# One step's issue order in a fused causal attention and soft-MoE kernel: first scores and maxima's transpose to the front, attention products to the end

## The chip, the cores and the metric

The kernel runs on one core of a Trainium2 chip. The metric is device time in microseconds (us) of one execution. A core has a tensor engine (TensorE; PE in the profile, its weight loads PEld), a vector engine (VectorE, DVE), a scalar engine (ScalarE, ACT), GpSimd (POOL) and a queue that issues DMAs (SyncE, SP). Each engine takes its instructions in the order of the program and waits on semaphores for what the others make. SBUF is the on-chip memory, PSUM the memory that TensorE writes to; it has eight banks of 2 KB a partition.

## The reference

Causal attention over 8 batches of 12 heads, 448 positions, head dimension 64; then a soft mixture of experts over the 3584 tokens with 32 slots and 8 experts.

```python
scores = q @ k^T / sqrt(64)            # above the diagonal: -1e9
attn   = softmax(scores); x = attn @ v # x as (3584, 768)
logits = x @ phi                       # (3584, 32)
d = softmax(logits, over tokens); slot_input = d^T @ x
slot_out[e] = relu(slot_input[e] @ w1[e]) @ w2[e]
out = softmax(logits, over slots) @ slot_out
```

## The kernel before

There are 96 heads, taken in 48 pairs. The main loop (line 510) has one step i a head; h is 0 in even steps and 1 in odd ones, p is the pair. A step works on four heads at once, at different stages, and the order in which it issues their parts is written out by hand in the tuple ORDER (line 47), one row for even steps and one for odd ones; the loop walks it (line 539). Since every engine is in order, the place of a name in ORDER says what it stands behind on its own engine, and nothing else. These are the names, by engine:

- TensorE: c0, c3, c12 and k0 to k3 are the first scores of head i+2, a causal mask and four passes into a PSUM tile s of two banks (scores1). mr0 is the transpose of the maxima of head i+1 into the tile rt (max_row). t0 to t3 are four more passes into the tile s of head i, which add the rounding remainder of q and take off the row's maximum (scores2). a0 to a3 are the attention products of head i-1: ten products of 128x128 by 128x65 into the one tile po, two passes each (attv).
- VectorE: x0 to x3 find the maxima of head i+2 in blocks, first with one large transposing reduction over s (x0), then with three small elementwise maxima inside the tile r (max_keys). mr1 reduces rt to the row maxima mr of head i+1. n0 to n2 divide the product of head i-1 by its sum and write it to x (norm).
- GpSimd: sp spreads mr over the remainder tile r2 (max_spread). sk, in even steps, and sq, in odd ones, take the rounded copy off k and q of pair p+2, 64x896 values each (sub_k, sub_q).
- ScalarE: exp makes the probabilities pt of head i. ck and cq (even steps) make the rounded copies ks and qd of pair p+2, c2 (odd steps) copies ks to k2. ld takes the exponentials of a batch's logits.

The name plan runs what is due in the step from a table of due steps (line 433). Twelve steps are a batch. In a batch there are six transposes of x, one a pair (xtrans: four TensorE transposes into a tile xt, one ScalarE copy); three logits items (sixteen small TensorE passes into g, then lt on VectorE, in the third also the batch's maximum bm and the running maximum run_m); one item with the transposes of the exponentials and logits and three ScalarE instructions (logits_e); and two dispatches (eight TensorE passes into sp, one VectorE instruction into si).

The tiles s have three buffers, so the first scores of head i+2 wait for exp of head i-1. The tiles rt, xt, g, tp and sp share a single PSUM bank (misc, line 209): each waits until the one before it in the program has been read. po is one tile as well.

SP loads the queries and keys of pair p+3 and the values of pair p+1 at the head of an odd step (lines 512 to 516), into buffers that sk and sq set free, and one tile of expert weights in every second odd step. The loop is followed by the end of the attention, then by the experts and the output, whose weights are loaded while they run.

Of the kernel before, what the change touches and what calls it, by code (L numbers as in the profile page):

```python
# [20 lines left out]
PPB = NH // 2  # L21
# [23 lines left out]


ORDER = (
# [4 lines left out]
)  # L52

SC0, SC1, SC2, SC3 = 512, 0, 320, 960
# [30 lines left out]
def attention_soft_moe(ctx: ExitStack, tc: tile.TileContext, qk, va, phi, w1, w2, out):  # L85
# [39 lines left out]
    def load_qk(p, a, hs=slice(0, 2)):  # L125
        if p < NPAIR:
            if hs.start == 0:

                st["raw", a, p] = (wres.tile([P, 2 * WN], F32, tag="w", name=f"qk{a}_{p}")[:, 0:2 * S]
                                   .rearrange("p (h s) -> p h s", h=2)  # L130
                                   if (p, a) in ((1, 0), (2, 1)) else
                                   raw.tile([P, 2, S], F32, tag="qk", name=f"qk{a}_{p}"))
            nc.sync.dma_start(out=st["raw", a, p][:, hs], in_=qk[p, :, a, hs])

    def loads_v(p, eng=nc.sync):
        if p < NPAIR:
            eng.dma_start(out=va_[p % 2], in_=va[p])
# [28 lines left out]
    def load_w(n):  # L166
        if n < len(order):
            m, e, h, u = order[n]
            t = wtiles[order[n]] = slot(n, f"w{n}")
            src, q = (w1 if m == 0 else w2)[e, h], place(n)  # L170
            if n <= NBUF or q >= RES - 1:
                nc.sync.dma_start(out=t, in_=src[:, WN * u:WN * u + WN])
            elif u:

                nc.sync.dma_start(out=twos[n - q, q // 2], in_=src)
# [33 lines left out]
    def misc(name):  # L209
        return ps_1.tile([P, 512], F32, tag="m", name=name)  # L210
# [61 lines left out]
    def scores1_all(i):  # L272
        for part in ("c0", "k3", "c3", "c12", "k2", "k1", "k0"):
            scores1(i, part)
# [36 lines left out]
    def scores2(i, cs):  # L311
        if i >= NHD:
            return
        p, h = divmod(i, 2)
        s = st["s", i]
        k2, r2 = k2_, r2_[p % NR]
        for c in cs:
            w, m = S - CQ0[c], min(P, S - P * c)
            nc.tensor.matmul(s[0:m, SCOL[c]:SCOL[c] + w], k2[:, h, P * c:P * c + m],
                             r2[:, h, CQ0[c]:S], start=False, stop=True, skip_group_check=True)  # L320
# [41 lines left out]
    def xtrans(p):  # L362
        x = st.pop(("x", p))
        pt = misc(f"xt{p}")
        for c in range(NCH):
            nc.tensor.transpose(out=pt[:, P * c:P * c + P], in_=x[:, c], identity=ident)
        xt = st["xt", p] = xtp.tile([P, 512], F32, tag="xt", name=f"xts{p}", bufs=2)
        nc.scalar.activation(out=xt, in_=pt, func=AF.Copy)
# [13 lines left out]
    def logits_b(b, l):  # L382
        bm = st["bm", b] = moe.tile([P, 1], F32, tag="bm", name=f"bm{b}", bufs=2)
        nc.vector.tensor_reduce(out=bm, in_=l, axis=AX.X, op=ALU.max, negate=True)

        mo, mn = run_m[(b + 1) % 2], run_m[b % 2]
        nc.vector.tensor_tensor(out=mn, in0=mo, in1=st.pop(("bm", b)), op=ALU.min)

    def logits_d(b, l):
        mo, mn = run_m[(b + 1) % 2], run_m[b % 2]  # L390
        al = st["al", b] = moe.tile([P, 1], F32, tag="al", name=f"al{b}", bufs=2)
        bs = st["bs", b] = moe.tile([P, 1], F32, tag="bs", name=f"bs{b}", bufs=2)
        nc.scalar.activation(out=gs, in_=l, func=AF.Exp, bias=mn[:, 0:1], accum_out=bs)
        nc.scalar.activation(out=al, in_=mo, func=AF.Exp, scale=-1.0, bias=mn[:, 0:1])
# [5 lines left out]
    def logits_e(b):  # L400
        tp = misc(f"tp{b}")
        nc.tensor.transpose(out=tp[:, 0:P], in_=gs, identity=ident)
        nc.tensor.transpose(out=tp[:, P:2 * P], in_=lt, identity=ident)
        st["dn", b] = gs.rearrange("p (c s) -> p c s", s=NSLOT)
        nc.scalar.activation(out=gs, in_=tp[:, 0:P], func=AF.Copy)
        nc.scalar.activation(out=lg[:, b], in_=tp[:, P:2 * P], func=AF.Copy)
        nc.scalar.activation(out=run_z, in_=run_z, func=AF.Identity, scale=st["al", b][:, 0:1],
                             bias=st.pop(("bs", b))[:, 0:1])
# [15 lines left out]
    def next_logits(b, j, m):  # L424
        logits_a(b, (j, j + 1), m[:, 0:P])
        logits_t(j, m[:, 0:P])

    def dispatch(b, hf):
        sp = misc(f"sp{b}_{hf}")
        dispatch_a(b, hf, sp)  # L430
        dispatch_b(b, hf, sp)

    plan = {}
    for b in range(NB):
        o, last = 12 * b, b == NB - 1
        for j, r in enumerate((3, 5, 9, 10, 12, 13)):
            if not last or j < PPB - 2:
                plan[o + r] = lambda p=b * PPB + j: xtrans(p)
        for j, r in ((0, 8), (2, 11)):
            plan[o + r] = lambda b=b, j=j: next_logits(b, j, misc(f"g{b}_{j}"))  # L440
        if not last:
            plan[o + 14] = lambda b=b: (next_logits(b, 4, misc(f"g{b}_4")), logits_b(b, lt))
            plan[o + 16] = lambda b=b: logits_e(b)
            plan[o + 18] = lambda b=b: dispatch(b, 0)
            plan[o + 19] = lambda b=b: dispatch(b, 1)

# [63 lines left out]
    for i in range(NHD):  # L510
        p, h = divmod(i, 2)
        if h:
            load_qk(p + 3, 1)
            if p + 1 < NPAIR - 1:
                loads_v(p + 1)
            load_qk(p + 3, 0)
            if p % 2 and nload < RES:
                load_w(nload)
                nload += 1
        if i == NHD - 3:  # L520

            loads_v(NPAIR - 1, nc.scalar)
        if i < 2:
            scores2(i, (1, 0, 2))
            if i:
                scores1_all(3)
            scores2(i, (3,))
            exps(i)
            if i == 0:
                max_row(1, 0)  # L530
                warm(START[4], po0.rearrange("p a b->p (a b)")[:, 0:P])
                max_row(1, 1)
                sub_k(1, h1, nc.vector)
                max_spread(1)
                sub_q(1, h1)

        qs = [int(n[1]) for n in ORDER[h] if n[0] == "a"]
        first = qs[:2] if qs[0] == 3 else qs[:1]
        for n in ORDER[h]:
            if i < 2 and (n == "exp" or n[0] in "kt" or n in ("c0", "c3", "c12")):  # L540
                continue
            if i == 0 and n in ("mr0", "mr1", "sp"):
                continue
            if n[0] == "k" or n in ("c0", "c3", "c12"):
                scores1(i + 2, n)
            elif n[0] == "t":
                scores2(i, (int(n[1]),))
            elif n[0] == "a":
                attv(i - 1, (int(n[1]),), first)
            elif n[0] == "x":  # L550
                max_keys(i + 2, int(n[1]))
            elif n[0] == "n":
                norm(i - 1, int(n[1]))
            elif n in ("mr0", "mr1"):
                max_row(i + 1, int(n[2]))
            elif n == "ld":
                if i % 12 == 3 and i > 12:
                    logits_d(i // 12 - 1, lt)
            elif n == "plan":
                if later and i:  # L560
                    later.pop(0)()
                plan.get(i, int)()
            else:
                {"exp": lambda: exps(i), "sp": lambda: max_spread(i + 1),
                 "ck": lambda: cast_k(p + 2), "sk": lambda: sub_k(p + 2), "cq": lambda: cast_q(p + 2),
                 "c2": lambda: copy_k2(p + 1), "sq": lambda: sub_q(p + 2)}[n]()
        if i == NHD - 1:

            scs.close()
            pe = att.enter_context(tc.tile_pool(name="pe", bufs=1, space=PSUM, reuse_waits="tile"))  # L570
            ps = [pe.tile([P, 512], F32, name=f"e{k}") for k in range(6)]

    i, b, p = NHD - 1, NB - 1, NPAIR - 1
# [68 lines left out]
    for hf in range(2):  # L642
        tps = po0.rearrange("p a b->p (a b)")[:, 0:96] if hf == 0 else ps[2][:, 0:96]
        for c in range(3):
            o = 384 * hf + P * c
# [153 lines left out]
    n = NBUF  # L799
# [83 lines left out]
```

## Time and profile before

| | us |
|---|---|
| median of three runs | 467.58 |
| lowest and highest run | 467.29 and 470.31 |
| profiled execution | 467.8 |
| its span, first to last instruction | 466.0 |
| busy ScalarE, of the span | 288.5 |
| busy GpSimd, of the span | 266.7 |

All numbers of the profile are of that one execution. In a row of a timeline stand the start in us from the span's start, the duration, the engine, a line (here always a helper's, L69, so that groups are told apart by the tiles), the operation, its output and inputs, their shapes and the count; in brackets the idle time ahead of it and what ended it. The chain of waits has the start, the duration and the engine with its tile. A group's row ends with its busy time, the mean duration in ns, and its idle time. A matmul's row includes the time in which it drains, which overlaps the next one.

### The profile page before, as it was taken

To read this page: it belongs to the slowest core of one execution; us is meant where nothing else is said; L and a number is where in the kernel's file an instruction comes from. 1 tells how busy PE (TensorE), PEld (TensorE's weight loads), DVE (VectorE), ACT (ScalarE), POOL (GpSimd) and SP (SyncE) were. 2 spreads that over 40 slices of the span, in tenths; PEclk is the share of its full clock that TensorE was granted. 3 is DMA by queue.
4 is the path that set the end of the run, shared out by engine and by line. 5 is a ranking of instruction groups with operands and counts; after the bars stand their busy time and mean duration, and the time that the engine had idled before them with its cause. 6 is when DMAs were issued, how large, how long until landed. Compare 5 with 4: busy or idle time off the path is not lost.

```text
span 466.0 us, 11818 instructions
## 1 busy us (share of the span) xinstructions
PE 429.8 (92%) x4628; PEld 368.3 (79%) x4628; DVE 338.5 (73%) x954; ACT 288.5 (62%) x400; POOL 266.7 (57%) x216
## 2 busy tenths in 40 slices
PE   7799999999999999999999999999999999899850
PEld 3688998898999899988998899889988864454430
DVE  6888788878787888788788877887888447634350
ACT  5576777577767777777677677767774411243240
POOL 5788777776777677767776777677765100000000
PEclk9999999999999999999999999999999999999995
DMA  7376666765676656755676656765667999999998
GB/s 265 105 244 218 201 220 210 234 210 183 207 244 234 208 181 211 239 207 190 213 245 224 201 184 219 229 227 184 232 210 243 403 367 426 423 422 413 404 391 346
DMA packets 34471, 119.02 MB, mean 255 GB/s; under 512 B 3824, under 2 KB 8944, under 8 KB 32880
## 3 DMA queue, kind: packets, MB, share of 16 engines
q1 hardware_dynamic: 34272, 118.01, 71.8%
q8 instruction: 36, 0.59, 0.5%
q10 hardware_dynamic: 144, 0.27, 0.2%
q14 instruction: 19, 0.16, 0.1%
HBM read 107.25 MB, written 11.01 MB: 254 GB/s over the span
## 4 chain that ended last, share of the span: by engine, by line
PE 69%; DVE 14%; DMA 12%; issue 1%; ACT 1%; SPq 0%
PE po L69 31%; PE s L69 21%; DMA w<-in_w_dram 11%; DVE r L69 7%; PE xt L69 5%; PE sp L69 2%; DVE run_m L69 2%; PE g L69 2%; PE rt L69 2%; PE pp L69 1%; PE e L69 1%; DVE x L69 1%; DVE sm L69 1%; PE hp L69 1%; DMA qk<-in_qk_dram 1%
## 5 line engine op out<-in xcount | busy, mean ns | idle before, releaser
L69 PE MATMUL po<-va,pt 128*128 128x65 f32 x1900 | 193.3, 250 | 0.2 <-ACT xts L69 0.2
L69 PEld LDWEIGHTS po<-va,pt 128*128 128x128 f32 x1900 | 190.6, 170 | 0.5 <-ACT xts L69 0.4
L69 ACT ACTIVATE pt<-s 128x1024 f32<-128x1024 f32 x96 | 98.4, 1025 | 87.0 <-PE s L69 84.5
L69 DVE TRANSPOSE_TENSOR_REDUCE r<-s 128x32 f32<-128x1024 f32 x96 | 119.9, 1249 | 26.5 <-PE s L69 23.9
L69 POOL TENSOR_SCALAR_AFFINE_SELECT r<-mr 14x448 fp32r<-14x448 f32 x96 | 62.1, 646 | 86.9 <-DVE mr L69 60.4
L69 POOL TENSOR_TENSOR r<-qk,qd 64x896 fp32r<-64x896 f32 (+1 forms) x50 | 101.4, 2027 | 6.6 <-ACT qd L69 2.8
L69 POOL TENSOR_TENSOR ks<-qk,ks 64x896 fp32r<-64x896 f32 (+1 forms) x47 | 97.7, 2080 | 3.7
L69 PE MATMUL s<-r,k 128*128 128x320 f32 (+3 forms) x384 | 82.9, 297 | 2.2 <-POOL r L69 2.1
L69 PE MATMUL s<-qd,ks 128*128 128x448 f32 (+3 forms) x384 | 76.0, 308 | 0.9 <-ACT qd L69 0.8
L69 DVE TENSOR_TENSOR r<-r 128x10 f32<-128x10 f32 (+2 forms) x288 | 58.7, 204 | 9.8
L69 PEld LDWEIGHTS s<-r,k 128*128 128x128 f32 (+1 forms) x384 | 59.9, 176 | 5.8 <-POOL r L69 3.5
L69 PEld LDWEIGHTS s<-qd,ks 128*128 128x128 f32 (+1 forms) x384 | 55.1, 181 | 2.4 <-ACT qd L69 1.8
L69 ACT ACTIVATE ks<-qk 128x896 fp32r<-128x896 f32 (+1 forms) x50 | 45.7, 916 | 3.9 <-DMA qk<-in_qk_dram 2.7
L69 ACT ACTIVATE k<-ks 64x896 fp32r<-64x896 f32 (+1 forms) x49 | 45.8, 935 | 1.2
L69 ACT ACTIVATE qd<-qk 128x896 fp32r<-128x896 f32 (+1 forms) x50 | 45.7, 913 | 0.4 <-DMA qk<-in_qk_dram 0.3
L69 DVE TENSOR_TENSOR x<-po,sm 128x256 f32<-128x256 f32 x95 | 40.3, 425 | 3.3
L69 PEld LDWEIGHTS <-identb 128*128 128x128 bf16 x339 | 29.2, 99 | 16.5 <-issue 14.7
L69 PE MATMUL s<-tri,identb 128*128 128x64 bf16 (+2 forms) x288 | 39.8, 235 | 0.0
L69 PE MATMUL xt<-ident,x 128*128 128x128 f32 x188 | 29.9, 282 | 7.7 <-DVE mr L69 7.4
L69 ACT ACTIVATE xts<-xt 128x512 f32<-128x512 f32 x47 | 28.1, 597 | 11.5 <-PE xt L69 9.7
L69 DVE TENSOR_SCALAR sm<-po 128x4 f32<-128x4 f32 x95 | 15.1, 159 | 23.1 <-PE po L69 22.7
L69 DVE TENSOR_REDUCE mr<-rt 14x32 f32<-14x128 f32 x96 | 26.7, 278 | 2.5 <-PE rt L69 2.2
(135 smaller groups left out, 365.9 us busy)
## 6 DMA issues: line engine op xcount, KB each, us to landing
qk<-in_qk_dram SPq DMA_DIRECT2D x94, 448.0 KB, 3.3
w<-in_w_dram SPq DMA_DIRECT2D x43, 768.0 KB, 6.3
w<-in_w_dram SPq DMA_DIRECT2D x10, 1536.0 KB, 18.9
va<-in_va_dram SPq DMA_DIRECT2D x47, 260.0 KB, 3.4
out_dram<-ot SPq DMA_DIRECT2D x16, 384.0 KB, 6.7
out_dram<-ot SPq DMA_DIRECT2D x2, 1536.0 KB, 9.2
qk<-in_qk_dram SPq DMA_DIRECT2D x4, 224.0 KB, 3.4
hw<-in_w_dram SPq DMA_DIRECT2D x1, 768.0 KB, 6.3
```

The lines of the kernel that those rows point to most:

```text
L69: return self._tc.keep_in_program_order(op(*args, **kwargs))
```

## The change

The two rows of ORDER are written anew. On each engine:

- TensorE: first scores, then mr0 (before: among the attention products), then t0 to t3 without a break (before: t3 behind a3, or a3 and t3 apart), then what is new under pa, then a0 to a3 in one block (before: a0 and a3 ahead of mr0, a2 and a1 behind it), then plan.
- VectorE: mr1, x0 to x3, n0 to n2, plan (before: x0 to x3, mr1, n0 to n2, plan).
- GpSimd: sp, then sk or sq, the same order as before. sp follows mr1, which now stands ahead of x0.
- ScalarE, even steps: ck, exp, pa, cq, ld (before: ck, exp, cq, ld, plan). Odd steps: exp, c2, pa, ld (before: exp, ld, c2, plan).

The name pa runs a second table, plan_a, to which the six transposes of x and logits_e move; logits and dispatches stay in plan at the step's end. No instruction is added, removed or resized.

```diff
 ORDER = (
-    ("c3", "c0", "k3", "c12", "k1", "k0", "k2", "t0", "t2", "t1", "a0", "a3", "t3", "ck",
-     "mr0", "exp", "x0", "a2", "x1", "x2", "x3", "mr1", "a1", "cq", "sp", "n0", "sk", "n1", "ld", "n2", "plan"),
-    ("c3", "c0", "k3", "c12", "k0", "k1", "k2", "t0", "t1", "t2", "a0", "x0", "t3", "a3", "exp", "mr0",
-     "x1", "x2", "x3", "mr1", "sp", "a2", "a1", "n0", "ld", "n1", "n2", "sq", "c2", "plan"),
+    ("ck", "c3", "c0", "k3", "c12", "k1", "k0", "k2", "mr0", "mr1", "sp", "sk", "t0", "t2", "t1", "t3", "exp", "pa",
+     "x0", "x1", "x2", "x3", "cq", "a0", "a1", "a2", "a3", "n0", "n1", "n2", "ld", "plan"),
+    ("c3", "c0", "k3", "c12", "k0", "k1", "k2", "mr0", "mr1", "sp", "t0", "t1", "t2", "t3", "sq", "exp", "c2", "pa",
+     "x0", "x1", "x2", "x3", "a0", "a1", "a2", "a3", "n0", "n1", "n2", "ld", "plan"),
 )
...
-    plan = {}
+    plan, plan_a = {}, {}
...
-                plan[o + r] = lambda p=b * PPB + j: xtrans(p)
+                plan_a[o + r] = lambda p=b * PPB + j: xtrans(p)
...
-            plan[o + 16] = lambda b=b: logits_e(b)
+            plan_a[o + 16] = lambda b=b: logits_e(b)
...
+            elif n == "pa":
+                plan_a.get(i, int)()
             elif n == "plan":
```

## The prediction

> **What bounds the kernel now.** I read the page first (span, engine shares, the chain), then busy time by stage, the chain in order of time over two batches, the waits, and last the timelines of VectorE (DVE) and GpSimd (POOL) one by one.
>
> ```profile
> span 466.0 us, 11818 instructions
> ...
> PE 429.8 (92%) x4628; PEld 368.3 (79%) x4628; DVE 338.5 (73%) x954; ACT 288.5 (62%) x400; POOL 266.7 (57%) x216
> ...
> PE 69%; DVE 14%; DMA 12%; issue 1%; ACT 1%; SPq 0%
> ```
> ```profile
> 200.00:240.00 40.00, 38.97 (x425) 36.10 (x425) 32.29 (x96) 29.34 (x38) 29.05 (x23) 1.00 0.65 217
> ...
> 400.00:466.00 66.00, 45.65 (x408) 23.95 (x400) 23.79 (x54) 20.30 (x49) 0.00 (x0) 0.90 0.99 399
> ```
> The columns of the second view are the stage, its length, busy time of PE, weight load, DVE, ACT and POOL, granted clock, DMA share, GB/s. In the loop TensorE is busy 38.97 of 40 us; after it DMA is full (0.99), and the change leaves that stage and its bytes alone. So what the loop loses or gains goes one for one into the span.
>
> ```profile
> 161.10 0.66 PE xt L69 x4
> ...
> 194.52 1.14 PE s L69 x10
> 195.66 0.19 PE po L69 x2
> 195.85 0.03 PE s L69
> 195.88 0.50 PE po L69 x8
> 196.38 0.11 PE rt L69
> 196.49 1.06 PE po L69 x10
> 197.56 0.48 PE xt L69 x4
> 198.03 1.17 PE s L69 x10
> ...
> 199.98 1.08 PE po L69 x10
> ...
> 205.73 0.04 issue
> 205.77 0.66 PE xt L69 x4
> ```
> ```profile
> PEld xt L69 <- DVE mr L69: 9.8, 16, 1.2
> ```
> ```profile
> L69 DVE TENSOR_TENSOR run_m<-run_m,bm x7: 1284/1285/1303, 68.2 to 336.5; 128x1 f32<-128x1 f32 x7
> ```
> The chain in order of time shows a step of nothing but TensorE: from 194.52 to 198.03, 3.51 us. Two like points one batch of twelve steps apart, 161.10 and 205.77, give 44.67 us a batch, 3.72 a step. In between, once a batch, the chain leaves TensorE: the last product stands at 199.98, and the transpose of x at 205.77 waits for the maxima's reduction (mr). The row of waits prices it at 1.2 us at most (9.8 us in all); the row of run_m, seven of them, says it comes seven times.
>
> **The change, by engine, and its price.** The row of a batch's stall first, in VectorE's own order (start, duration):
>
> ```profile
> 201.50 0.42 DVE L69 TENSOR_TENSOR x<-po,sm 128x256 f32<-128x256 f32 x1
> 201.84 0.28 DVE L69 TENSOR_TENSOR lt<-g,lt 128x128 f32<-128x128 f32 x1
> 202.15 0.29 DVE L69 TENSOR_REDUCE bm<-lt 128x1 f32<-128x128 f32 x1
> 202.47 1.28 DVE L69 TENSOR_TENSOR run_m<-run_m,bm 128x1 f32<-128x1 f32 x1
> 203.68 1.24 DVE L69 TRANSPOSE_TENSOR_REDUCE r<-s 128x32 f32<-128x1024 f32 x1
> 204.95 0.56 DVE L69 TENSOR_TENSOR r<-r 128x10 f32<-128x10 f32 x3
> 205.44 0.28 DVE L69 TENSOR_REDUCE mr<-rt 14x32 f32<-14x128 f32 x1
> 205.65 0.14 DVE L69 TENSOR_SCALAR sm<-po 128x4 f32<-128x4 f32 x1
> ...
> 206.03 0.43 DVE L69 TENSOR_TENSOR x<-po,sm 128x256 f32<-128x256 f32 x1
> ```
> ```profile
> 201.64 2.10 POOL L69 TENSOR_TENSOR ks<-qk,ks 64x896 fp32r<-64x896 f32 x1
> 205.79 0.64 POOL L69 TENSOR_SCALAR_AFFINE_SELECT r<-mr 14x448 fp32r<-14x448 f32 x1 [2.05 <-DVE sm L69]
> 206.51 2.11 POOL L69 TENSOR_TENSOR r<-qk,qd 64x896 fp32r<-64x896 f32 x1
> ```
> A one-column run_m takes 1.28 us and ends at 203.75; POOL's subtraction ends at 203.74. That is a wait on POOL, not work. The same early in the loop with x1, the first of the three small maxima that follow the large transposed one (x0):
>
> ```profile
> 43.05 1.58 DVE L69 TENSOR_TENSOR r<-r 128x10 f32<-128x10 f32 x1
> ```
> ```profile
> 42.51 2.09 POOL L69 TENSOR_TENSOR r<-qk,qd 64x896 fp32r<-64x896 f32 x1
> ```
> ```profile
> 44.95 0.28 DVE L69 TENSOR_REDUCE mr<-rt 14x32 f32<-14x128 f32 x1
> ```
> ```profile
> L69 DVE TENSOR_TENSOR r<-r 128x6 f32<-128x6 f32 x54 | 9.0, 166 | 1.9
> ...
> L69 DVE SCALAR_TENSOR_TENSOR si<-si,al,sp 128x384 f32<-128x384 f32 x8 | 4.9, 615 | 0.2
> ```
> x1 should cost about what x2 costs, 0.17 us; it takes 1.58 and ends at 44.63, POOL's subtraction at 44.60. Both blocked instructions read two SBUF operands. The row at 201.50, with one operand in PSUM, keeps its 0.42 us although POOL's subtraction starts inside it. The Trainium skill, page "SBUF — State Buffer", section "Who interferes with whom", says that a DVE instruction with two SBUF inputs and a GpSimd instruction that reads SBUF exclude one another, and that the one issued later waits for the whole of the other. The trace agrees for VectorE as the later one, in the two places above; no row there shows POOL as the later one. By that rule the sum below stays as it is, and it is issue order that decides it.
>
> POOL and VectorE together: the term that decides. Before, mr and with it the spread (sp) and the subtraction (sk or sq) stand behind x1 to x3, so the subtraction runs over the normalisation and the next x0, and is just over when the next x1 comes. The change puts mr ahead of x0. Count from the start of mr, by the rows from 205.44: sp starts at 0.35, the subtraction at 1.07 and ends at 3.18 (206.51 plus 2.11). VectorE starts x0 at 0.21, and x1 1.27 later (203.68 to 204.95), so at 1.48. That is 0.41 inside the subtraction, which is there in every step: sk in even steps, sq in odd ones. x1 is held to 3.18. From there the rest of x1, x2 and x3 take 0.35 (44.60 to 44.95), the three normalisation instructions 0.38 from first to third (205.65 to 206.03) and the third 0.34 until the next may start (201.50 to 201.84). The next mr stands behind them on VectorE: 3.18 + 0.35 + 0.38 + 0.34 = 4.25 us a step. TensorE's 3.51 fits inside, so VectorE and POOL become the bound. Queued behind x1 are x2, x3, the normalisation, the plan's item and the next mr; the next maxima's transpose on TensorE waits for x3, and the transpose of x for mr.
>
> What the plan's items add. The scratch bank that rt needs is now released by the item before it. A logits item adds lt behind the normalisation (0.28), then release, transpose and hand-over. The transpose's row is this:
> ```profile
> L69 PE MATMUL rt<-ident,r 128*14 128x128 f32 x53 | 14.5, 275 | 0.0
> ```
> With 0.04 for each hand-over (the row at 205.73), that is 0.28 + 0.04 + 0.28 + 0.04 = 0.64, twice a batch. The third one has bm and run_m behind lt: 0.31 + 0.32 (201.84 to 202.47) and a run_m that finds POOL idle, taken at 0.17 like x2: 0.80. A dispatch item has 0.615 in place of 0.28: 0.97, twice. The x transposes add nothing: ACT empties that bank under the next first scores. Sum 2 x 0.64 + 0.80 + 2 x 0.97 = 4.02 a batch.
>
> TensorE. Of the twenty narrow passes a step, ten take 1.06, or 0.106 each, behind a rt of 0.11 that covers their first weight load. In the new order all twenty follow the last subtracted pass (0.03), too short to cover it, or a transpose of x (0.48), which does. One load more in the open costs up to 0.11 a step, nothing where x is transposed there; the widest block of score passes gains from standing together by at most the same. I take +0.05 if TensorE is the bound, and nothing here, since it has 4.25 - 3.51 = 0.74 to spare; without that cover it costs 0.05 x 91 = 4.6 us. The old stall (1.2 us, seven times) goes, for the transpose of x no longer waits behind run_m, x0 and the three maxima; what is late in its place is x1.
>
> ACT, SP, and the moved copies. exp, the k2 copy, the two casts and the copies of transposed x only change places on ACT, which is busy 62%; cq comes behind one copy more, and its reader (sq) runs a step later. If that cover went, it would be one copy in one step of two. The loads on SP's queue are not in the order; their buffers come free at the end of sk and sq, which stay 3.18 behind mr, and the row
> ```profile
> qk<-in_qk_dram SPq DMA_DIRECT2D x94, 448.0 KB, 3.3
> ```
> says 3.3 us to land, under a step of 4.25, with the reader more than a step away. Cost nothing from either side.
>
> Sum. A batch: 12 x 4.25 + 4.02 = 55.02 against 44.67, so +10.35. Subtractions are issued in steps 1 to 91. Steps 12 to 91 are 80/12 batches: +69.0. Steps 1 to 11 hold two logits items and no dispatch: (4.25 + 2 x 0.64/11 - 3.72) x 11 = +7.1. Together +76 on the profiled execution, which took 467.8 (span 466.0 and 1.8 around it): 543.8. That execution is 0.2 above the median of the three runs, so I say 543.6.
>
> **Rivals.** It gets faster. Mechanism: sk and sq start after x1 has started, and then POOL waits some 0.2 us for it and VectorE for nothing. The point from which it decides: the subtraction must start more than 1.48 behind mr instead of 1.07. Then the old stall goes and TensorE pays 4.6: 467.8 - 7 x 1.2 + 4.6 = 464.0; with the load hidden after all, 459.4. Nothing in the rows delays the subtraction by 0.41, since its operands are cast a step earlier. Only one step in two is held. If sk had to wait for its cast or load in even steps, these would stay near TensorE's (44.67 - 1.2)/12 = 3.62 and odd ones take 4.25; with half of the 4.02 a batch is 6 x 3.62 + 6 x 4.25 + 2.01 = 49.2, +4.6 a batch over 91/12 batches: 503. Against it: the landing time above, and a longer step gives the cast more room. Held, and longer still. If VectorE's small instructions follow one another end to start, not overlapped, the three places where I took an overlap (mr to x0 is under POOL's time; x3, normalisation, next mr) cost about 0.2 more a step: +18, 562. A lower clock would belong here too; the loop stood at 1.00, and TensorE would still be busy some 3.5 of 4.6 us.
>
> **How the numbers follow.** The held x1 in every step has 0.84, one step in two 0.06, not held 0.10 (0.04 faster by over 1%, 0.06 within). About 1% is what a measurement here can tell from no change. The forecast is that of the likeliest case, 544. Its own range goes from 0.17 a step less (the seven small instructions between x1 and the next mr close up by the length of one: 528) to the end-to-start case and a little clock (568). That leaves out the other two cases, 0.16, and little else. Slower by over 1%: 0.90; within: 0.06; faster: 0.04.
>
> **What would show it.** Right: x1's rows lengthen from about 0.2 us to some 1.6 and each ends with a POOL subtraction; run_m falls from 1.28 to about 0.2; batches stand 55 us apart; the longest waits in the loop are TensorE's for VectorE (rt for r, xt for mr), and its busy share in the loop falls from 97% to about 80%. Wrong: x1 short while the subtraction runs, a subtraction that starts behind x1, or mr waiting for TensorE and not for the normalisation.

## The result, and the profile after

The changed kernel takes 547.66 us (median; 546.21 to 548.26) against 467.9 for the kernel before (median of four runs), a ratio of 1.169 with a 95% interval of 1.164 to 1.174. It is slower by 80 us, and the forecast was 543.6. The profiled execution has a span of 546.1 us.

The page of the changed kernel: engine shares, then VectorE's costliest group (busy time, mean in ns, idle time ahead).

```profile
PE 458.9 (84%) x4628; PEld 373.2 (68%) x4628; DVE 450.0 (82%) x954; ACT 288.3 (53%) x400; POOL 265.5 (49%) x216
...
L69 DVE TENSOR_TENSOR r<-r 128x10 f32<-128x10 f32 (+2 forms) x288 | 192.1, 667 | 9.8
```

No instruction was added, yet VectorE's busy time rises from 338.5 to 450.0 us. The three small maxima alone go from 58.7 to 192.1 us. A held instruction shows as busy, not as idle: this is why the two engine shares alone do not tell work from waiting. By shape, in the stretch from 100 to 400 us of the changed kernel:

```profile
L69 DVE TENSOR_TENSOR r<-r 128x10 f32<-128x10 f32 x66 | 113.6, 1721 | 2.3
...
L69 DVE TENSOR_TENSOR r<-r 128x6 f32<-128x6 f32 x65 | 10.8, 166 | 2.2
L69 DVE TENSOR_TENSOR r<-r 128x2 f32<-128x2 f32 x65 | 10.5, 161 | 2.2
```

Only x1 (128x10) grew; x2 and x3 cost what they did. Two steps of VectorE's timeline, then GpSimd's, both of the changed kernel:

```profile
199.27 1.23 DVE L69 TRANSPOSE_TENSOR_REDUCE r<-s 128x32 f32<-128x1024 f32 x1
200.54 1.72 DVE L69 TENSOR_TENSOR r<-r 128x10 f32<-128x10 f32 x1
```
```profile
202.57 0.16 DVE L69 TENSOR_SCALAR sm<-po 128x4 f32<-128x4 f32 x1
...
203.31 0.27 DVE L69 TENSOR_REDUCE mr<-rt 14x32 f32<-14x128 f32 x1
203.51 1.23 DVE L69 TRANSPOSE_TENSOR_REDUCE r<-s 128x32 f32<-128x1024 f32 x1
...
208.59 0.28 DVE L69 TENSOR_REDUCE mr<-rt 14x32 f32<-14x128 f32 x1 [0.44 <-PE rt L69]
208.79 1.23 DVE L69 TRANSPOSE_TENSOR_REDUCE r<-s 128x32 f32<-128x1024 f32 x1
```
```profile
200.14 2.09 POOL L69 TENSOR_TENSOR r<-qk,qd 64x896 fp32r<-64x896 f32 x1
```

x1 starts at 200.54 and ends at 202.26; POOL's subtraction started at 200.14 and ends at 202.23. From one x0 to the next is 203.51 - 199.27 = 4.24 us in a step with no dearer plan item, and 208.79 - 203.51 = 5.28 in one with a dispatch. The batch is read from run_m, which comes once in each:

```profile
L69 DVE TENSOR_TENSOR run_m<-run_m,bm x7: 158/158/160, 80.3 to 411.6; 128x1 f32<-128x1 f32 x7
```

(411.6 - 80.3)/6 = 55.22 us a batch, where before it was (336.5 - 68.2)/6 = 44.72. run_m itself takes 0.16 us and no longer 1.28, since POOL is idle when it comes (of one batch, run_m starts at 246.02; POOL's subtraction ended at 244.31 and its next instruction starts at 246.45). The two longest waits of TensorE for VectorE in the changed kernel are these (total, times, longest):

```profile
PEld rt L69 <- DVE lt L69: 24.8, 20, 1.3
...
PEld rt L69 <- DVE si L69: 19.3, 14, 1.4
```

They are the shared bank: in a step behind a logits or dispatch item, rt waits until lt, or the dispatch's write to si, has read it.

### The profile page after: what moved, and what is told of

It is laid out like the page before. It is cut to its first block, busy times and chain, and to the rows that moved or that the text cites. A ratio compares the mean times of both kernels' runs of the same rounds, so it can differ in the third digit from the quotient of the medians.

```text
span 546.1 us, 11816 instructions
## 1 busy us (share of the span) xinstructions
PE 458.9 (84%) x4628; PEld 373.2 (68%) x4628; DVE 450.0 (82%) x954; ACT 288.3 (53%) x400; POOL 265.5 (49%) x216
## 5 line engine op out<-in xcount | busy, mean ns | idle before, releaser
L69 DVE TENSOR_TENSOR r<-r 128x10 f32<-128x10 f32 (+2 forms) x288 | 192.1, 667 | 9.8
L69 PE MATMUL po<-va,pt 128*128 128x65 f32 x1900 | 188.9, 255 | 0.5 <-issue 0.5
L69 PEld LDWEIGHTS po<-va,pt 128*128 128x128 f32 x1900 | 181.9, 172 | 2.8 <-issue 0.6
L69 DVE TRANSPOSE_TENSOR_REDUCE r<-s 128x32 f32<-128x1024 f32 x96 | 117.9, 1228 | 0.1
L69 PE MATMUL rt<-ident,r 128*14 128x128 f32 x96 | 26.5, 276 | 58.6 <-DVE lt L69 20.3
L69 PE MATMUL s<-r,k 128*128 128x320 f32 (+3 forms) x384 | 70.2, 304 | 0.5 <-POOL r L69 0.5
L69 PEld LDWEIGHTS rt<-ident,r 128*14 128x14 f32 x96 | 8.4, 88 | 78.7 <-DVE lt L69 24.8
L69 PEld LDWEIGHTS s<-r,k 128*128 128x128 f32 (+1 forms) x384 | 54.7, 177 | 2.3 <-POOL r L69 0.7
L69 PEld LDWEIGHTS <-identb 128*128 128x128 bf16 x339 | 26.8, 99 | 15.9 <-issue 14.8
```

The lines of the kernel that those rows point to most:

```text
L69: return self._tc.keep_in_program_order(op(*args, **kwargs))
```

## The experiments

All ratios are to the kernel before, run beside them on the same chip. The edits are shown as changes to ORDER, only the names that matter.

**Only mr, sp and the subtraction ahead of x0.** Attention products, transposes of x and casts stay where they were before.

```diff
-  ... k2 t0 t2 t1 a0 a3 t3 ck mr0 exp x0 a2 x1 x2 x3 mr1 a1 cq sp n0 sk ...
+  ... k2 mr0 mr1 ck sp sk t0 t2 t1 a0 a3 t3 exp x0 a2 x1 x2 x3 a1 cq n0 ...
```

> The reverse: only the maxima's transpose, mr, sp and the subtraction move ahead of x0; attention products, transposes of x and the rest keep the places they had before. The lock says x1 is held to the end of the subtraction, some 1.6 to 1.8 us in each step, a batch of some 55 us, 540 to 555 in all. If the order of the attention products were the cost, this would stand near the time before, at most 480.

Measured: 548.06 us, ratio 1.168 (1.163 to 1.174). x1 has a mean of 1722 ns and a batch is 55.18 us. This part alone makes the whole loss; the blocks of attention products and the second plan table are not needed for it.

**The reverse: TensorE's new order, maxima ahead of mr again.**

```diff
-  ... mr0 mr1 sp sk t0 t2 t1 t3 exp pa x0 x1 x2 x3 cq a0 a1 a2 a3 n0 n1 n2 ld plan
+  ... mr0 t0 t2 t1 t3 exp x0 x1 x2 x3 mr1 sp sk cq a0 a1 a2 a3 n0 n1 n2 pa ld plan
```

> TensorE keeps its new order up to the attention products; on VectorE the four maxima come ahead of mr again, with sp and the subtraction behind mr, and the transposes of x go back to the step's end. If VectorE is held by POOL's subtraction (the lock), x1 falls back to about 0.2 us and the time to 464 to 474, with a batch near 45 us. If the new place of TensorE's blocks is what costs, the time stays above 520 and x1 has nothing to do with it.

Measured: 483.02 us, ratio 1.031 (1.027 to 1.036). x1 is back at 175 ns. The loss is mostly gone, but the time misses the expected range by 9 us. The chain, the waits and run_m of this kernel say where the rest is:

```profile
205.14 0.28 PE rt L67
...
205.88 1.84 PE po L67 x20
```
```profile
PEld rt L67 <- ACT xts L67: 11.9, 45, 0.9
```
```profile
L67 DVE TENSOR_TENSOR run_m<-run_m,bm x7: 950/953/956, 73.7 to 352.1; 128x1 f32<-128x1 f32 x7
```

The twenty narrow passes in one block take 1.84 us; set apart as before they took 0.19 + 0.50 + 1.06 = 1.75 in an odd step and 0.64 + 1.06 = 1.70 in an even one, so the block costs 0.09 and 0.14. And rt, now early in the step, waits for ACT to copy the transposed x of the step before out of the shared bank: in the step shown it takes 0.28 us of the chain, and 0.11 before. Last, run_m is still held by POOL's subtraction, at 0.95 us (its row at 212.89 ends at 213.85, POOL's subtraction at 213.83), so the old stall has not gone either. A batch is (352.1 - 73.7)/6 = 46.40 us.

**The changed order with late casts.** Only ACT's order changes: the subtraction then has to wait for its operand.

```diff
-  even: ck ... mr0 mr1 sp sk t0 t2 t1 t3 exp pa x0 ... cq a0 ...
+  even: ... mr0 mr1 t0 t2 t1 t3 exp ck sp sk pa x0 ... a0 ...
-  odd:  ... t3 sq exp c2 pa ...
+  odd:  ... t3 exp cq sq c2 pa ...
```

> The changed order as it is on TensorE, VectorE and GpSimd; only ACT's casts move: ck behind exp, and cq to the odd step behind exp, ahead of c2. The subtraction then has to wait for its cast and starts some 2.4 us behind mr instead of 1.07, after the small maxima (1.48 to 2.05). The lock says that x1 is short, and the time 462 to 475. If the order itself is the cost (mr ahead of x0 on VectorE, or the shared bank), it stays within 1% of 547; if a late subtraction holds something else, it is above.

Measured: 499.21 us, ratio 1.065 (1.061 to 1.070); a batch of 48.60 us. x1 takes 170 ns, so it is free, and 48 us of the 80 are gone with TensorE's and VectorE's order untouched. But the time is above the expected range. One part of the rest is the hold itself, once a batch on the last of the small maxima (x3, 128x2):

```profile
221.53 1.94 DVE L67 TENSOR_TENSOR r<-r 128x2 f32<-128x2 f32 x1
```
```profile
221.35 2.10 POOL L67 TENSOR_TENSOR r<-qk,qd 64x896 fp32r<-64x896 f32 x1 [0.71 <-ACT qd L67]
```
```profile
L67 DVE TENSOR_TENSOR r<-r 128x2 f32<-128x2 f32 x60 | 18.6, 309 | 2.0
```

x3 ends at 223.47, the subtraction at 223.45. In the group (100 to 340 us, five batches) the mean of 309 against 161 ns is 8.9 us too much, or 1.8 a batch; run_m, at 0.88 us, adds 0.7. That is up to 2.5 of the 3.4 us by which this batch is longer than that of the next experiment (45.17). The other part is ACT: in this kernel it is late with the copy of transposed x, behind exp, cast and c2, and rt waits for it (both rows are one wait, seen by the weight load and by the pass):

```profile
PEld rt L67 <- ACT xts L67: 17.7, 24, 0.9
PE rt L67 <- ACT xts L67: 11.6, 24, 0.6
```

**The subtractions replaced by work that only writes.** Each subtraction from pair 2 on becomes three memsets of the same area, in the changed order; this kernel leaves out the remainders of k and q.

```diff
-            (eng or nc.gpsimd).tensor_tensor(out=ks, in0=..., in1=ks, op=ALU.subtract)
+            for _ in range(3): nc.gpsimd.memset(ks.bitcast(F32), 0.0)
```

> The changed order, with each subtraction of the loop (pair 2 onward) replaced by three memsets of the same area, 0.84 us each by the profile before: POOL is as long at work at the same place, but only writes. The remainders of k and q are left out. If what holds x1 is POOL reading SBUF beside an instruction with two SBUF inputs, x1 falls to about 0.2 us and the time to 462 to 485. If any work of POOL holds it, x1 ends with one of the memsets, and the time stays above 520. If the order and not POOL is the cost, it stays at 547.

Measured: 470.96 us, ratio 1.006 (1.004 to 1.009). GpSimd is at work during the small maxima, and they are free:

```profile
202.55 0.57 DVE L69 TENSOR_TENSOR r<-r 128x10 f32<-128x10 f32 x3
```
```profile
202.13 2.64 POOL L69 MEMSET ks<- 64x896 f32 x3
```

All three maxima take 0.57 us inside memsets that run from 202.13 to 204.77. So it is not GpSimd's being busy, and not the order by itself. The Trainium skill, page "SBUF — State Buffer", section "Who interferes with whom", says that a VectorE instruction with two SBUF inputs contends with a GpSimd instruction that reads SBUF, not with one that only writes it. The traces agree: 0.57 us here against 2.12 for the same three beside a subtraction. This kernel also shows what the new order is worth without the hold: TensorE is busy 39.64 of 40 us, and a batch takes (340.4 - 69.4)/6 = 45.17 us:

```profile
200.00:240.00 40.00, 39.64 (x422) 35.84 (x420) 30.74 (x92) 28.63 (x38) 33.11 (x43) 1.00 0.60 204
```
```profile
L69 DVE TENSOR_TENSOR run_m<-run_m,bm x7: 159/160/163, 69.4 to 340.4; 128x1 f32<-128x1 f32 x7
```

**Subtractions in halves.**

```diff
-  "sk": lambda: sub_k(p + 2), ... "sq": lambda: sub_q(p + 2)
+  "sk": lambda: [sub_k(p + 2, q) for q in (h0, h1)], ... "sq": lambda: [sub_q(p + 2, q) for q in (h0, h1)]
```

> The changed order, each subtraction in two instructions of half the size (some 1.05 us each, from 1.07 behind mr). The lock holds x1 to the end of the first half, about 2.15, not 3.18. Then it turns on who is first: if x2 and x3 come before the second half, the step is near 3.7 us and the time 470 to 490; if the second half comes first and holds x2 or x3 to some 3.3, the step is 4.3 to 4.5 and the time 545 to 560. With any other cause the halves change nothing, 547.

Measured: 542.35 us, ratio 1.158 (1.154 to 1.163), 3 us under the range given for the second half coming first. By shape, from 100 to 340 us:

```profile
L69 DVE TENSOR_TENSOR r<-r 128x6 f32<-128x6 f32 x53 | 56.5, 1066 | 1.8
L69 DVE TENSOR_TENSOR r<-r 128x10 f32<-128x10 f32 x52 | 39.8, 766 | 1.8
L69 DVE TENSOR_TENSOR r<-r 128x2 f32<-128x2 f32 x53 | 8.5, 161 | 1.8
```

One step of VectorE, then of GpSimd:

```profile
202.35 0.77 DVE L69 TENSOR_TENSOR r<-r 128x10 f32<-128x10 f32 x1
...
203.15 1.06 DVE L69 TENSOR_TENSOR r<-r 128x6 f32<-128x6 f32 x1
```
```profile
201.95 1.14 POOL L69 TENSOR_TENSOR ks<-qk,ks 64x448 fp32r<-64x448 f32 x1
...
203.05 1.15 POOL L69 TENSOR_TENSOR ks<-qk,ks 64x448 fp32r<-64x448 f32 x1
```

x1 is held by the first half only (0.77 and not 1.72; it ends at 203.12, the half at 203.09), and then x2 by the second (it ends at 204.21, the half at 204.20). The second half starts at 203.05, x2 at 203.15: the half is ahead, so only 5 of the 80 us are won. The hold moves with the size of the subtraction, in the way a lock for the length of one instruction does.

**The smaller term: the shared bank.** Two ways were tried. The first put rt into spare columns of po's bank, as a part of the tile po, with the changed order and with the late casts.

```diff
-            st["rt", i] = misc(f"rt{i}")
+            st["rt", i] = pob[:, 384:512]
```

> The changed order, with the maxima's transpose rt in the spare columns of the bank of po, so that it no longer waits for the shared bank. This tests the smaller term: the plan's items would add only VectorE's own time (0.28 or 0.62 and not 0.64 or 0.97). A batch gets some 1.4 to 1.8 us shorter, 53.5 to 53.9 us, and the time falls to 532 to 538; x1 stays held at 1.7. If the bank is not what the items cost, 546 to 549.

> The late casts, and rt in columns of its own. The late casts alone came to 499 with x1 free (0.17 us) and a new wait of rt for the copy of transposed x on ACT. If that wait is what kept it above 475, the batch of 48.6 us falls to 45 to 46 and the time to 470 to 480. If the casts hold something else (the second scores, or the first ones of the next pair), it stays above 490.

Measured: 570.75 us (1.219; 1.214 to 1.223) and 508.94 us (1.087; 1.084 to 1.091), both slower than without: the first lies in neither of its ranges, the second in the one above 490. As part of the tile po, rt now waits for the normalisation that reads po, in nearly every step of the first and in about every second step of the other. In the waits of the first of the two (100 to 380 us; rt counts as po there) the row is

```profile
PEld po L69 <- DVE x L69: 64.9, 57, 1.6
```

One wait was put in place of another, so these two say nothing about the bank. The second way moves the plan's item ahead of the attention products, on VectorE ahead of the normalisation:

```diff
-  ... x0 x1 x2 x3 cq a0 a1 a2 a3 n0 n1 n2 ld plan
+  ... x0 x1 x2 x3 cq plan a0 a1 a2 a3 n0 n1 n2 ld
```

> The changed order with the plan's items (logits, dispatch) moved from the step's end to the place ahead of the attention products, on VectorE ahead of the normalisation. The shared bank is then read out before rt wants it, and an item costs only VectorE's own time: three times lt at 0.31, bm and run_m 0.45, two dispatches at 0.62, 2.6 us a batch and not some 4. If the release of the bank is the smaller term of the sum, the batch goes from 55.2 to 53.5 us and the time to 532 to 537, with x1 held as before. If the bank does not matter, 545 to 549.

Measured: 532.12 us, ratio 1.135 (1.127 to 1.143). The batch falls from 55.22 to (395.8 - 77.9)/6 = 52.98 us, with x1 still held at 1717 ns. The bank's late release is the smaller term, and even 0.5 us a batch more went than expected. The longest wait of rt for lt falls from 1.3 to 0.5 us, for si from 1.4 to 0.6.

```profile
L67 DVE TENSOR_TENSOR run_m<-run_m,bm x7: 158/160/160, 77.9 to 395.8; 128x1 f32<-128x1 f32 x7
```

**The kernel before with one operand less.** The same hold makes the once-a-batch stall of the kernel before. Here run_m is a minimum against a column scalar.

```diff
-        nc.vector.tensor_tensor(out=mn, in0=mo, in1=st.pop(("bm", b)), op=ALU.min)
+        nc.vector.tensor_scalar(out=mn, in0=mo, scalar1=st.pop(("bm", b))[:, 0:1], scalar2=None, op0=ALU.min)
```

> The kernel before, with run_m made by a minimum against a column scalar, so that it has one SBUF tensor as input and not two. If two SBUF inputs are what makes it wait for POOL, run_m takes about 0.16 us and not 1.28, the transpose of x no longer waits, and up to 1.1 us go in each of seven batches: 459.5 to 463. If run_m waits for something of its own operands, it stays at 1.28 and the time at 467 to 468.5. If the column scalar is a second input as well, the same.

Measured: 461.11 us, ratio 0.983 (0.980 to 0.987): 1.7% faster than the kernel before. A second run of the same kernel, beside the last experiment, agrees.

> The same kernel as the one with run_m against a column scalar, once more beside the one with the product set apart: 460 to 462.

Measured: 461.51 us, ratio 0.983 (0.978 to 0.987).

```profile
L69 DVE TENSOR_SCALAR run_m<-run_m,bm x7: 213/216/217, 69.8 to 331.5; 128x1 f32<-128x1 f32 x7
```

```profile
200.79 0.21 DVE L69 TENSOR_SCALAR run_m<-run_m,bm 128x1 f32<-128x1 f32 x1
```
```profile
199.94 2.10 POOL L69 TENSOR_TENSOR ks<-qk,ks 64x896 fp32r<-64x896 f32 x1
```

run_m takes 0.22 us (median) with POOL's subtraction running, from 199.94 to 202.04 in the batch shown, and a batch takes (331.5 - 69.8)/6 = 43.62 us.

**One product more set apart.** On that kernel, a1 stands between t0 and the next pass.

```diff
-  ... k2 t0 t2 t1 a0 a3 t3 ... a2 ... a1 ...
+  ... k2 t0 a1 t2 t1 a0 a3 t3 ... a2 ...
```

> The order before with run_m against a column scalar (461 alone), and one attention product more set apart: a1 between the passes t0 and the next. A narrow pass behind a wide one has its weight load covered, 0.05 to 0.1 us a step; with TensorE the bound that is 456 to 458. If the product has to wait there for the normalisation of the head before (po), or the load is not covered, 460 to 466.

Measured: 466.05 us, ratio 0.994 (0.991 to 0.997), slower than the 461 beside it and not the 456 to 458 expected. A batch takes (334.1 - 68.2)/6 = 44.32 us, 0.70 more. The chain of this kernel shows, in one step,

```profile
206.87 0.04 PE s L67
206.92 0.02 issue
206.94 1.03 ACT pt L67
207.97 0.04 issue
208.01 1.07 PE s L67 x8
```

a1's passes (0.39 us) now stand ahead of exp, and with six narrow passes and not ten behind t3 in an even step, the first scores of the next step wait here for exp to free their buffer. This is not so in every step: the chain goes through exp twice a batch, in the odd step with ld and in the even one behind it. In the others TensorE stays the bound and nothing is won: in a whole even step (from 211.69) the narrow passes take 0.39 + 0.64 + 0.62 = 1.65 us and not the 1.70 of the 461 kernel, but the score passes, now in three groups, 0.92 + 0.31 + 0.03 = 1.26 and not 1.18 + 0.03 = 1.21.

## Why the prediction was right

- *The held x1, 4.25 us a step.* Measured 4.24. Each part of it stands in the rows after: the subtraction runs when x1 comes, x1 ends 0.03 behind it, and the next mr starts behind the normalisation. It is held in every step and not in every second one: a mean of 1721 ns in 66 rows, the longest of them 1731, leaves room for no short one. Removing the hold on x1 from the changed order in three ways (maxima first, late casts, memsets) took 65, 48 and 77 us of the 80 away, and in the first two some of the rest is the same hold on run_m and x3; adding it alone to the order before gave all 80.
- *The plan's items, 4.02 us a batch.* A batch of 55.22 less 12 x 4.24 leaves 4.34. A dispatch was priced at 0.97 and took 5.28 - 4.24 = 1.04. A logits item was priced at 0.64 and the third at 0.80; each took 0.72 in most batches (4.96 from x0 to x0). Moving the items showed that the release of the bank is in this term.
- *The whole.* 10.35 us a batch were forecast, 55.22 - 44.72 = 10.50 came. The first run_m is 80.3 - 68.2 = 12.1 us late, where the forecast gave 7.1 to the first eleven steps and some 0.86 to each step after, 9.7 up to there. These two make up most of the 4 us by which the time exceeds the forecast.
- *TensorE's own order, +0.05 a step if it were the bound.* Too small. The block of twenty passes costs 0.09 in an odd step and 0.14 in an even one, and without the hold a batch takes 45.17 us against the 43.62 of the kernel before without its stall, 0.13 a step. It was hidden as forecast, under VectorE and GpSimd.
- *The rival that would be faster.* Its condition did not occur, and its time was off as well. With the hold taken out (memsets in place of the subtractions) the changed order gives 471, not 464: it is no gain even then, because TensorE pays more for its new order (0.13 x 12 = 1.6 us a batch) than the old stall cost (44.72 - 43.62 = 1.1).
- *The busy share of TensorE* was put at about 80% of the loop; from 100 to 400 us it is 256.8 of 300, 86%. Of the two waits named as signs, rt for r and xt for mr, neither is the longest: rt does wait for VectorE, but mostly for lt and si, which hold the shared bank (24.8 and 19.3 us), and xt waits for mr only 6.3 us in all, at most 0.5 at a time.

What stays open: how much of the 0.13 belongs to the narrow block's weight loads and how much to rt's early place, which in two experiments made it wait for ACT; it was not taken apart further.

## What to carry to other kernels

On engines that run in order, moving a short reduction forward also moves what it releases on another engine. Ask what that engine then does at the same time, operand by operand: here a VectorE instruction with two tensors in SBUF lost up to 1.8 us where it fell into a 2.1 us GpSimd instruction that reads SBUF, and before the change the small maxima missed it in most steps (x1 209 ns on average from 100 to 300 us). A VectorE instruction that was too long for its size in a group's row was, in all of these cases, waiting, though it counts as busy; look for a GpSimd row that ends when it ends, and then take one tensor operand away (a column scalar did for run_m) or move one of the two.

## What the runs showed of the hardware that was not expected

With halves, the waiting x1 went on when GpSimd's first half ended, but the second half, next in GpSimd's queue, started ahead of x2: x1 took 0.77 and x2 1.07 us on average. Splitting the GpSimd instruction therefore split the hold and hardly shortened it. A column scalar out of SBUF did not count as a second tensor here: run_m went from 1.28 to 0.22 us at the same place, though the operation changed with it, from tensor_tensor to tensor_scalar.
